# Attention by clusters and two feed-forward layers: a new order of units around the change of layers, and three roundings on another engine

## The chip, the cores and the metric

The program runs on one core of a Trainium2 chip. The metric is the device time of one execution in microseconds (us). The kernel before took 785.29, 785.1 and 782.73 us in three runs, median 785.1.

Engines are named as in the profile: PE is the matrix engine, DVE the vector engine, ACT the scalar engine, POOL is GpSimd, SP issues the DMAs.

## The reference

What is computed is an attention in which a query sees the keys of its own cluster alone, then two feed-forward layers on its 1536 rows of 512. Layer 2 normalizes its input and gates it.

```python
mask = q_assign[:, :, :, None] == k_assign[:, :, None, :]
scores = np.where(mask, scale * np.matmul(q, k.transpose(0, 1, 3, 2)), -1e9)
x = softmax(scores) @ v                      # 1536 rows of 512
h = x @ w_in                                 # layer 1: 512 to 2048
g = where(h >= 1, h, where(h <= -1, 0, (h + 1) ** 2 / 4))
x = g @ w_out                                # 2048 to 512
xn = x / sqrt(mean(x * x) + 1e-6) * rms_g    # layer 2
g = xn @ w_gate                              # 512 to 1536
out = (g / (1 + exp(-g)) * (xn @ w_val)) @ w_out
```

## The kernel before, in words

Every float32 product is made of three passes in a faster format. Each operand is split into a high part, rounded, and a low part, the remainder (`hi` and `low` in `rounded`, for a gated tile of 128 x 512). A product is high by high, high by low and low by high. Weights arrive in full and are split by DVE and ACT in six steps each (`conv_ops`), one step at a time between other work.

Tokens stand in three blocks b of 512, or twelve tiles t of 128. Hidden columns stand in slices m of 128, 16 in layer 1 and 12 in layer 2. Units of work on PE:

- `h_unit` (h): 12 matmuls of 512 columns, one slice m for one block b. ACT and DVE apply the gate, and `rounded` splits the result: high on ACT, low on DVE.
- `y_unit` (y): the second product of a group of slices for one tile of tokens, 9 matmuls for a group of three. DVE adds it to Y. The last group of layer 1 (n = 4, slices 13 to 15) also has ACT sum its squares.
- `norm_r` and `norm_y` (`norm` and `scale` in `units`): eleven small DVE instructions for a block's 1/rms, and one for each tile that scales Y.
- `turn_pair(t)` (pair): eight transposes, of tiles t and t + 4. ACT and DVE then make XH and XL, the high and low parts of layer 2's input, and three sums of the two blocks; the lows of these and of one quarter of the input are four instructions on POOL (L763).
- `turn_unit(t)` (turn): four transposes for a tile of block 2, with its high part on ACT and its low part on DVE (L865).

In layer 2, blocks 0 and 1 are multiplied by a scheme with seven products in place of eight. `term_unit(k, m)` is one of them, 6 matmuls, k from 1 to 7. Terms 1, 6, 7 and 4 add up in one accumulator B; ACT copies it away (u, v, w) between two of them, and the next may start only when the copy is done. Terms 5 and 3 share E, term 2 fills A. Terms 5 and 6 use the first of two sums of weights, 3 and 7 the second. These are made on POOL and split in two steps each. Block 2 takes the plain way (`one_unit`): `one(0, m)` is the gate product, `one(1, m)` the value product, 12 matmuls each. `slice_of(m)` lists, with the places freed left out: 1, 5, one(0), 2, 6, one(1), 3, 7. Term 4 of a slice (`last_of`) follows inside the next slice.

The order of units is written out by hand in `units`. Each engine executes its instructions in the order of the program. At the start of a unit `drain` issues the work behind the units before it, by stages, and `fill` adds steps of weight splitting as the planned times of PE and DVE allow (second and third entry of a unit). So a unit that is moved also moves its ACT, DVE and POOL work, and can move weight splitting and its loads. Weights pass through two load buffers: a load on SP waits until the splitting of the slice two before it is through.

Products and transposes share six banks of the accumulator memory in rotation (`HB`); a unit waits until the bank of six tiles before is read.

The hand order at the change of layers, layer 1's last group and layer 2's first slices:

Of the kernel before, what the change touches and what calls it, by code (L numbers as in the profile page):

```python
# [9 lines left out]
F32 = mybir.dt.float32  # L10
# [3 lines left out]
ALU = mybir.AluOpType  # L14
# [9 lines left out]
M1, M2 = FF1 // 128, FF2 // 128  # L24
TOK = B * S
BLK = 512
NB = TOK // BLK
GROUPS1 = [3, 3, 4, 3, 3]
# [12 lines left out]
def clustered_attention_two_ffn(  # L41
# [14 lines left out]
    nc = tc.nc  # L56
# [414 lines left out]
    a, b, c = prep(0), prep(1), prep(2)  # L471
# [27 lines left out]
    fp = {"gp": []}  # L499
# [127 lines left out]
    def h_unit(layer, m, b):  # L627
        cs = slice(BLK * b, BLK * b + BLK)
        w = need((layer, 0, m))
        drain()  # L630
        h = fp["h"](f"h{layer}_{m}_{b}")
        proj(h, w, cs)
        a = fp["a"](f"a{layer}_{m}_{b}")

        fp["g", m, b] = a
        G[layer, m, b] = take()

        def gate():
            nc.scalar.activation(a, h, AF.Relu, bias=half_b, scale=0.5)  # L639
            nc.scalar.activation(a, a, AF.Square)  # L640
            nc.vector.scalar_tensor_tensor(a, h, 1.0, a, op0=ALU.max, op1=ALU.min)  # L641

        hi, low = rounded(layer, m, b)
        later.append((gate, lambda: (hi(), low())))
# [15 lines left out]
    def rounded(layer, m, b):  # L660
        g = G[layer, m, b]

        def low():
            nc.vector.tensor_tensor(g[:, 1], fp["g", m, b], g[:, 0].bitcast(F32), op=ALU.subtract)
            whole.add((layer, m, b))

        return lambda: nc.scalar.copy(g[:, 0], fp["g", m, b]), low
# [26 lines left out]
    def key_of(k, m):  # L694
        i = TERMS[k][1]
        return (2, i, m) if i >= 0 else (2, -1 - i, -m - 1)
# [72 lines left out]
    def y_unit(layer, n, t):  # L769
        groups = (GROUPS1, GROUPS2)[layer - 1]  # L770
        m0 = sum(groups[:n])
        ms = range(m0, m0 + groups[n])
        b, j = divmod(t, 4)
        fs = slice(128 * j, 128 * j + 128)
        ws = [need((layer, layer, m)) for m in ms]
        drain()

        n_cols = 2 if layer == 2 and n + 1 == len(groups) and t == 3 else 1
        cols = [slice(DM // n_cols * c, DM // n_cols * (c + 1)) for c in range(n_cols)]
        ys = [fp["y"](f"y{layer}_{n}_{t}_{c}") for c in range(n_cols)]  # L780
        for c, y in zip(cols, ys):
            for m, w in zip(ms, ws):
                assert (layer, m, b) in whole
                g = G[layer, m, b]
                nc.tensor.matmul(y[:, c], g[:, 0, fs], w[:, 0, c], start=(m == m0), stop=False)  # L785
                nc.tensor.matmul(y[:, c], g[:, 0, fs], w[:, 1, c], start=False, stop=False)  # L786
                nc.tensor.matmul(y[:, c], g[:, 1, fs], w[:, 0, c], start=False, stop=(m == ms[-1]))  # L787
        if j == 3:
            for m in ms:
                give(G.pop((layer, m, b)))  # L790
        if t == (4 * NB - 1, 3)[layer - 1]:
            for m in ms:
                give(W.pop((layer, layer, m)))
        Y = fp["Y"][:, t]

        def add():
            for c, y in zip(cols, ys):
                if n == 0:
                    nc.scalar.copy(Y[:, c], y[:, c])
                else:  # L800
                    nc.vector.tensor_tensor(Y[:, c], y[:, c], Y[:, c], op=ALU.add)  # L801
                    tick()
                if n + 1 == len(groups):
                    if layer == 1:
                        norm_sq(t)
                    else:
                        nc.sync.dma_start(out[128 * t:128 * t + 128, c], Y[:, c])

        later.append((add,))
# [59 lines left out]
    def release(layer, m):  # L869
        for i in range(layer):  # L870
            give(W.pop((layer, i, m)))
# [4 lines left out]
    def units():  # L876

        def h(layer, m, b):
            return (lambda: h_unit(layer, m, b), 2.77, 1.36, [(1, 0, m)], -1)

        def y(layer, n, t):
            groups = (GROUPS1, GROUPS2)[layer - 1]
            m0 = sum(groups[:n])
            return (lambda: y_unit(layer, n, t), 0.693 * groups[n], 0.68 if n else 0.0,
                    [(layer, layer, m) for m in range(m0, m0 + groups[n])],
                    groups[n] * ((t % 4 == 3) + (t == (4 * NB - 1, 3)[layer - 1])))

        def done(layer, m):
            return (lambda: release(layer, m), 0.0, 0.0, [], layer)

        def turn(t):
            return (lambda: turn_unit(t), 0.6, 0.68, [], 0)

        def norm(b):
            return (lambda: norm_r(b), 0.0, 1.0, [], 0)

        def scale(t):
            return (lambda: norm_y(t), 0.0, 0.68, [], 0)

        def term(k, m):  # L900
            return (lambda: term_unit(k, m), 1.36, {2: 0.6, 3: 0.6, 7: 1.2, 4: 1.2}.get(k, 0.0), [key_of(k, m)], -(k in (7, 4)))

        def one(i, m):
            return (lambda: one_unit(i, m), 2.72, 1.2 * i, [(2, i, m)], -i)

        def end(*keys):
            return (lambda: free_unit(keys), 0.0, 0.0, [], len(keys))

        def slice_of(m):
            g, v, s, r = (2, 0, m), (2, 1, m), (2, 0, -m - 1), (2, 1, -m - 1)  # L910
            return [term(1, m), term(5, m), one(0, m), term(2, m), end(g), term(6, m), end(s), one(1, m), term(3, m), term(7, m), end(r)]

        def last_of(m):
            return [term(4, m), end((2, 1, m))]

        def ys(layer, n, b=None):
            return [y(layer, n, 4 * k + j) for k in ((2, 1, 0) if layer == 2 else range(NB)) for j in range(4) if b in (None, k)]

        def hs(layer, ms, b):
            return [h(layer, m, b) for m in ms]  # L920

        def scales(b):
            return [scale(t) for t in range(4 * b, 4 * b + 4)]

        def pair(t):
            return (lambda: turn_pair(t), 0.9, 2.2, [], -6 * (t == 0))

        def mix(xs, zs):
            r = []
            for i, x in enumerate(xs):  # L930
                r += [x] + zs[len(zs) * i // len(xs):len(zs) * (i + 1) // len(xs)]
            return r

        yield from [h(1, m, b) for b in range(NB) for m in range(GROUPS1[0])]
        for m in range(GROUPS1[0]):
            yield done(1, m)
        for n in range(1, len(GROUPS1) - 1):
            m0, g = sum(GROUPS1[:n]), GROUPS1[n]
            ks = []
            for m in range(m0, m0 + g):  # L940
                ks += [[h(1, m, b)] for b in range(NB)]
                ks[-1].append(done(1, m))
            for b in range(NB):
                yield from ys(1, n - 1, b)
                if n == 2 and b == 0:
                    yield (tables, 0.0, 0.0, [], 0)
                for k in ks[g * b:g * b + g]:
                    yield from k
        n = len(GROUPS1) - 1
        new = range(sum(GROUPS1[:n]), M1)  # L950
        yield from (*ys(1, n - 1, 0), *hs(1, new, 0), *ys(1, n - 1, 1), *hs(1, new, 1), *ys(1, n, 0))
        yield from mix(ys(1, n, 1), [norm(0), *scales(0)])
        ws = ys(1, n - 1, 2)
        yield from (ws[0], norm(1), ws[1], scale(4), ws[2], scale(5), ws[3], scale(6), scale(7))
        hz, yz = hs(1, new, 2), ys(1, n, 2)
        yield from (pair(0), *hz, *(done(1, m) for m in new), pair(1), pair(2), yz[0], yz[1], pair(3), yz[2], yz[3])
        zs = scales(2)
        f, e = slice_of(0), slice_of(1)
        yield from (f[0], f[3], norm(2), f[1], f[5], zs[0], f[6], zs[1], f[8], zs[2], e[0], f[9], zs[3], f[10], turn(8), e[1], turn(9),
                    *last_of(0)[:1], turn(10), e[3], turn(11), e[5], e[6], f[2], f[4], e[8], f[7], *last_of(0)[1:], e[2], e[4], e[9], e[10], e[7])  # L960
        for n, size in enumerate(GROUPS2):
            m0 = sum(GROUPS2[:n])
            for m in range(max(m0, 2), m0 + size):
                x = slice_of(m)
                yield from (*x[:2], *(last_of(m - 1) if m > m0 else ()), *x[2:])
            zs = ys(2, n)
            yield from (zs[0], *last_of(m0 + size - 1), *zs[1:])

# [105 lines left out]
    done = {"values": 4, "rows": []}  # L1074
# [259 lines left out]
```

## Time and profile before

| | before |
|---|---|
| median of three runs | 785.1 us |
| profiled execution, its own time | 783.73 us |
| its span, first to last instruction | 781.9 us |
| DVE busy over the span | 603.4 us (77%) |
| ACT busy | 391.8 us (50%) |
| POOL busy | 284.2 us (36%) |
| granted PE clock in the 40 slices | 0.9 or more of full speed in all |

The profiled execution has 1.8 us around its span, and lies 1.4 us below the median. Of a group or row of the trace the numbers are: start and duration in us from the first instruction, the engine, the line of the kernel, the operation, what it writes and reads, and in square brackets how long the engine stood idle before it and what ended that.

### The profile page before, as it was taken

How to read it: one execution, taken by the hardware profiler on the slowest of the kernel's cores; microseconds unless marked ns; L12 is line 12 of the kernel's file. 1: busy time of each engine (PE TensorE's matmuls, PEld its weight loads, DVE VectorE, ACT ScalarE, POOL GpSimd, SP SyncE). 2: the span in 40 equal slices, each digit the busy share in tenths (PEclk: the TensorE clock that was granted, in tenths of full speed). 3: DMA queues.
4: the chain of work that ended last, by engine and by line, in shares of the span. 5: the costliest groups of instructions: out<-in, count | busy, mean ns of one | idle time of the engine just before them, and what ended most of it. 6: DMA issues, size and time to landing. Idle time of an engine off the chain costs nothing.

```text
span 781.9 us, 10858 instructions
## 1 busy us (share of the span) xinstructions
PE 769.5 (98%) x3714; PEld 592.5 (76%) x3714; DVE 603.4 (77%) x1109; ACT 391.8 (50%) x758; POOL 284.2 (36%) x310
## 2 busy tenths in 40 slices
PE   8999999999999999999999998889999999999998
PEld 4666676666568888888888887678888888888887
DVE  6777787776678998877668779888999778988643
ACT  6676667665657555443334435554444314423420
POOL 5878999998000000000003214423455133432300
PEclk9999999999999999999999999999999999999999
DMA  7657665582153776444333300135463234343003
GB/s 199 173 138 182 153 165 125 137 203 80 62 160 132 231 253 199 162 135 140 116 120 137 108 28 27 55 102 167 165 213 135 81 128 141 137 134 108 1 37 125
DMA packets 32679, 103.41 MB, mean 132 GB/s; under 512 B 5016, under 2 KB 5356, under 8 KB 32624
## 3 DMA queue, kind: packets, MB, share of 16 engines
q1 hardware_dynamic: 32612, 102.72, 43.2%
q8 instruction: 29, 0.48, 0.2%
q14 instruction: 26, 0.21, 0.1%
q10 hardware_dynamic: 12, 0.00, 0.0%
HBM read 81.02 MB, written 3.15 MB: 108 GB/s over the span
## 4 chain that ended last, share of the span: by engine, by line
PE 93%; DVE 3%; ACT 2%; DMA 0%; issue 0%; POOL 0%; ACTq 0%; DVEq 0%
PE h L624 25%; PE y L785 9%; PE y L786 9%; PE y L787 9%; PE pv L406 8%; PE B L651 7%; PE mp L336 5%; PE sc L385 4%; PE sc L386 4%; PE E L651 4%; PE A L651 2%; PE sum L425 1%; PE simt L171 1%; PE sum L414 1%; PE warm L78 1%; DMA bb<-oht 0%
## 5 line engine op out<-in xcount | busy, mean ns | idle before, releaser
L338 DVE TENSOR_REDUCE M<-mp 128x1 f32<-128x384 f32 x186 | 94.6, 552 | 44.6 <-PE mp L336 44.4
L398 POOL TENSOR_TENSOR acc<-acc,P 128x384 f32<-128x384 f32 x112 | 109.3, 1010 | 4.1 <-ACT P L388 3.5
L388 ACT ACTIVATE P<-sc 128x384 f32<-128x384 f32 x192 | 82.3, 490 | 42.0 <-PE sc L386 36.1
L534 POOL TENSOR_TENSOR bits<-place 128x256 f32<-128x256 f32 x10 | 9.1, 934 | 256.0 <-DVE place L580 256.0
L624 PE MATMUL h<-xh,aa 128*128 128x512 f32 x312 | 99.9, 390 | 0.1
L801 DVE TENSOR_TENSOR Y<-y,Y 128x512 f32<-128x512 f32 (+1 forms) x85 | 57.7, 681 | 41.2 <-PE y L787 40.7
L639 ACT ACTIVATE a<-h,half_b 128x512 f32<-128x512 f32 x48 | 33.0, 688 | 81.9 <-PE h L624 80.8
L406 PE MATMUL pv<-P,v 128*64 128x384 f32 x384 | 70.6, 492 | 0.0
L624 PEld LDWEIGHTS h<-xh,aa 128*128 128x128 f32 x312 | 58.6, 188 | 14.2 <-DVE a L641 0.8
L385 PE MATMUL sc<-aa,bb 112*128 112x384 f32 x192 | 66.0, 344 | 0.0
L386 PE MATMUL sc<-aa,bb 97*128 97x384 f32 x192 | 65.0, 339 | 0.0
L624 PE MATMUL h<-xh,bb 128*128 128x512 f32 x200 | 64.4, 389 | 0.0
L565 ACT ACTIVATE raw<-raw 128x512 f32<-128x512 f32 x62 | 41.9, 677 | 40.1 <-DMA raw<-w_gate 23.3
L624 PE MATMUL h<-xl,aa 128*128 128x512 f32 x156 | 60.7, 389 | 0.0
L641 DVE SCALAR_TENSOR_TENSOR a<-h,a 128x512 f32<-128x512 f32 x48 | 33.1, 690 | 30.4 <-ACT a L640 30.4
L336 PE MATMUL mp<-bb,aa 112*128 112x384 f32 x186 | 52.4, 359 | 0.5 <-DMA bb<-oht 0.2
L568 DVE SCALAR_TENSOR_TENSOR bits<-raw,bits 128x512 uint32<-128x512 uint32 x68 | 50.0, 735 | 1.2
L406 PEld LDWEIGHTS pv<-P,v 128*64 128x64 f32 x384 | 25.4, 136 | 31.4 <-issue 30.5
L336 PEld LDWEIGHTS mp<-bb,aa 112*128 112x128 f32 x186 | 32.3, 189 | 15.9 <-issue 5.5
L624 PEld LDWEIGHTS h<-xh,bb 128*128 128x128 f32 x200 | 37.6, 188 | 7.8
L534 POOL TENSOR_TENSOR bits<-aa 128x256 f32<-128x256 f32 x18 | 17.6, 998 | 62.3 <-DVE aa L580 59.0
L624 PE MATMUL h<-xl,bb 128*128 128x512 f32 x100 | 38.9, 389 | 0.0
(306 smaller groups left out, 1944.5 us busy)
## 6 DMA issues: line engine op xcount, KB each, us to landing
raw<-w_out SPq DMA_DIRECT2D x28, 512.0 KB
mid<-w_out SPq DMA_DIRECT2D x28, 511.8 KB
raw<-w_in SPq DMA_DIRECT2D x16, 512.0 KB
mid<-w_in SPq DMA_DIRECT2D x16, 511.8 KB
raw<-w_gate SPq DMA_DIRECT2D x12, 512.0 KB
raw<-w_val SPq DMA_DIRECT2D x12, 512.0 KB
mid<-w_gate SPq DMA_DIRECT2D x12, 511.8 KB
mid<-w_val SPq DMA_DIRECT2D x12, 511.8 KB
```

The lines of the kernel that those rows point to most:

```text
L336: nc.tensor.matmul(mp, A[0:112, h, 0, 128 * qt:128 * qt + 128], Bk[0:112, h, 0, HALF * n:HALF * n + HALF], start=True, stop=True)
L338: nc.vector.tensor_reduce(st["M2", p][:, j, n:n + 1], mp, axis=AX.X, op=ALU.max)
L385: nc.tensor.matmul(sc, Bk[0:112, h, 0, ks], A[0:112, h, 0, qs], start=True, stop=False)
L386: nc.tensor.matmul(sc, Bk[0:97, h, 1, ks], A[0:97, h, 1, qs], start=False, stop=True)
L388: nc.scalar.activation(P, sc, AF.Exp, scale=0.125)
L398: nc.gpsimd.tensor_tensor(acc, acc, P, op=ALU.add)
L406: nc.tensor.matmul(pv[64 * h:64 * h + 64, 0:HALF], st["v", p][:, h, kt], st["P", p, i, h], start=(kt == 0), stop=(kt == NT - 1))
L624: nc.tensor.matmul(h, w[:, wi, fs], x[:, kc, cs], start=(n == 0), stop=(n == 11))
L651: nc.tensor.matmul(h, w[:, wi, fs], x[xi][:, kc], start=start and n == 0, stop=(n == 5), skip_group_check=not start)
L785: nc.tensor.matmul(y[:, c], g[:, 0, fs], w[:, 0, c], start=(m == m0), stop=False)
L786: nc.tensor.matmul(y[:, c], g[:, 0, fs], w[:, 1, c], start=False, stop=False)
L787: nc.tensor.matmul(y[:, c], g[:, 1, fs], w[:, 0, c], start=False, stop=(m == ms[-1]))
```

## The change

Three things. Layer 1's last three low parts of block 2 (slices 13 to 15) are subtracted on POOL in place of DVE. The units between the last products of layer 1 and the first slices of layer 2 stand in another order: h of block 2 comes first, and the pairs stand between the y units. In every slice of layer 2 from the third on, term 5 moves from second place to behind one(0) and term 2.

```diff
         def low():
-            nc.vector.tensor_tensor(g[:, 1], fp["g", m, b], g[:, 0].bitcast(F32), op=ALU.subtract)
+            e = nc.gpsimd if layer == 1 and b == NB - 1 and m >= M1 - GROUPS1[-1] else nc.vector
+            e.tensor_tensor(g[:, 1], fp["g", m, b], g[:, 0].bitcast(F32), op=ALU.subtract)
...
-        ws = ys(1, n - 1, 2)
-        yield from (ws[0], norm(1), ws[1], scale(4), ws[2], scale(5), ws[3], scale(6), scale(7))
-        hz, yz = hs(1, new, 2), ys(1, n, 2)
-        yield from (pair(0), *hz, *(done(1, m) for m in new), pair(1), pair(2), yz[0], yz[1], pair(3), yz[2], yz[3])
+        hz, ws, yz = hs(1, new, 2), ys(1, n - 1, 2), ys(1, n, 2)
+        yield from (hz[0], norm(1), scale(4), scale(5), hz[1], scale(6), scale(7), hz[2], *(done(1, m) for m in new), pair(0), ws[0], pair(1), ws[1], ws[2],
+                    pair(2), ws[3], yz[0], pair(3), yz[1], yz[2], yz[3])
...
-        yield from (f[0], f[3], norm(2), f[1], f[5], zs[0], f[6], zs[1], f[8], zs[2], e[0], f[9], zs[3], f[10], turn(8), e[1], turn(9),
-                    *last_of(0)[:1], turn(10), e[3], turn(11), e[5], e[6], f[2], f[4], e[8], f[7], *last_of(0)[1:], e[2], e[4], e[9], e[10], e[7])
+        yield from (f[0], f[3], f[1], norm(2), f[5], zs[0], f[6], zs[1], f[8], zs[2], e[0], f[9], zs[3], f[10], turn(8), e[3], turn(9),
+                    turn(10), e[1], turn(11), e[5], e[6], *last_of(0)[:1], e[8], f[2], f[4], e[9], e[10], f[7], *last_of(0)[1:], e[2], e[4], e[7])
...
-                yield from (*x[:2], *(last_of(m - 1) if m > m0 else ()), *x[2:])
+                yield from (*x[:1], *(last_of(m - 1) if m > m0 else ()), *x[2:5], x[1], *x[5:])
```

In the names below, `a1_15_2` is layer 1's gated tile of slice 15, block 2; `h1_13_2` its product, `y1_4_8` the y unit of layer 1, group 4, tile 8; `h0_0_2` is one(0) of slice 0; `xt`, `t` and `v` belong to the turns; `B4` is the accumulator B of slice 4. The last number is a running one.

DVE in the kernel before, between the last two gates of layer 1 and slice 15's low part:

```order
L641 SCALAR_TENSOR_TENSOR a1_15_2_5044<-h1_15_2_5031,a1_15_2_5044 128x512
L664 TENSOR_TENSOR place4_3132<-a1_14_2_5025,place4_3132 128x512
L755 TENSOR_TENSOR t1_0_5060<-v1_5062,xt1_5050 128x256
L755 TENSOR_TENSOR t1_0_5060<-xt5_5055,t1_0_5060 128x256
L755 TENSOR_TENSOR t1_1_5061<-xt5_5055,v1_5062 128x256
L755 TENSOR_TENSOR t1_1_5061<-xt1_5050,t1_0_5060 128x256
L756 TENSOR_TENSOR xl_104<-xt1_5050,xh_103 128x4x128
L757 TENSOR_TENSOR xl_104<-xt5_5055,xh_103 128x2x128
L664 TENSOR_TENSOR aa1_107<-a1_15_2_5044,aa1_107 128x512
```

The three low parts now, on POOL (L665), ahead of the lows of the first pair:

```order
L534 TENSOR_TENSOR bits37_4573<-bb1_108 128x256
L665 TENSOR_TENSOR aa1_107<-a1_13_2_4896,aa1_107 128x512
L665 TENSOR_TENSOR bb1_108<-a1_14_2_4926,bb1_108 128x512
L665 TENSOR_TENSOR bb0_106<-a1_15_2_4947,bb0_106 128x512
L764 TENSOR_TENSOR xl_104<-t0_0_4963,xh_103 128x2x128
L764 TENSOR_TENSOR aa2_109<-t0_0_4963,bb1_108 128x2x128
```

The low part of slice 15 stood behind a turn's six instructions on DVE, and stands behind its own two fellows on POOL now.

PE before, from the last turn of block 2 to the first unit that reads it, one(0) of slice 0:

```order
L858 MATMUL xt11_5349<-ident_f_68,Y_3125 128x128 x4
L651 MATMUL B1_5274<-bb0_106,bb1_108 128x512
L651 MATMUL B1_5274<-bb1_108 128x512
L651 MATMUL B1_5274<-bb0_106,bb1_108 128x512 x2
L651 MATMUL B1_5274<-bb1_108 128x512
L651 MATMUL B1_5274<-bb0_106,bb1_108 128x512
L624 MATMUL h0_0_2_5372<-xh_103,place3_3131 128x512
L624 MATMUL h0_0_2_5372<-xl_104,place3_3131 128x512
```

The same stretch of PE now, with the later rows of each unit left out:

```order
L859 MATMUL xt11_5315<-ident_f_68,Y_3125 128x128 x4
L651 MATMUL B1_5244<-bb1_108,place5_3133 128x512
...
L651 MATMUL B0_5183<-aa1_107,bb0_106 128x512
...
L651 MATMUL E1_5304<-xh_103,bb2_110 128x512
...
L624 MATMUL h0_0_2_5360<-xh_103,place3_3131 128x512
L624 MATMUL h0_0_2_5360<-xl_104,place3_3131 128x512
```

One term stood between the last turn and its reader; three stand there now.

PE before in layer 2, from the end of term 7 of slice 3 over terms 1 and 5 of slice 4 to term 4 of slice 3:

```order
L651 MATMUL B3_5834<-aa2_109,bb2_110 128x512
L651 MATMUL B4_5958<-xh_103,place4_3132 128x512
L651 MATMUL B4_5958<-xl_104,place4_3132 128x512
L651 MATMUL B4_5958<-xh_103,place4_3132 128x512 x2
L651 MATMUL B4_5958<-xl_104,place4_3132 128x512
L651 MATMUL B4_5958<-xh_103,place4_3132 128x512
L651 MATMUL E4_5971<-xh_103,place1_3129 128x512
L651 MATMUL E4_5971<-xl_104,place1_3129 128x512
L651 MATMUL E4_5971<-xh_103,place1_3129 128x512 x2
L651 MATMUL E4_5971<-xl_104,place1_3129 128x512
L651 MATMUL E4_5971<-xh_103,place1_3129 128x512
L651 MATMUL B3_5834<-place0_3128,bb0_106 128x512
```

The same place on PE now:

```order
L651 MATMUL B3_5813<-aa0_105,place4_3132 128x512
L651 MATMUL B4_5933<-xh_103,aa2_109 128x512
L651 MATMUL B4_5933<-xl_104,aa2_109 128x512
L651 MATMUL B4_5933<-xh_103,aa2_109 128x512 x2
L651 MATMUL B4_5933<-xl_104,aa2_109 128x512
L651 MATMUL B4_5933<-xh_103,aa2_109 128x512
L651 MATMUL B3_5813<-aa1_107,bb1_108 128x512
```

Two terms stood between terms 7 and 4 of a slice, and one stands there now; the copy w of the accumulator falls into this stretch.

## Rows read from the trace of the kernel before

**Rows 1.** Waits of PE from 440 us on: us in total, times, longest.

```profile
PE h L624 <- DVE xl L865: 2.0, 1, 2.0
PE y L787 <- DVE aa L664: 2.0, 1, 2.0
PE B L651 <- DVE xl L756: 1.0, 1, 1.0
PE xt L858 <- DVE Y L851: 0.6, 1, 0.6
PE B L651 <- ACT w L712: 0.5, 1, 0.5
PE B L651 <- ACT u L712: 0.3, 1, 0.3
PE y L785 <- ACT aa L667: 0.2, 1, 0.2
```

**Rows 2.** PE in order of time, at the change of layers.

```profile
462.21 0.39 PE L785 MATMUL y<-bb,place 128*128 128x512 f32 x1
464.25 0.39 PE L785 MATMUL y<-bb,place 128*128 128x512 f32 x1
...
483.42 0.40 PE L786 MATMUL y<-aa,aa 128*128 128x512 f32 x1
485.77 0.50 PE L787 MATMUL y<-aa,aa 128*128 128x512 f32 x1 [1.96 <-DVE aa L664]
486.11 0.40 PE L785 MATMUL y<-aa,place 128*128 128x512 f32 x1
...
488.17 1.03 PE L741 MATMUL xt<-ident_f,Y 128*128 128x128 f32 x8
488.96 0.48 PE L785 MATMUL y<-aa,place 128*128 128x512 f32 x1
...
520.14 0.39 PE L624 MATMUL h<-xh,bb 128*128 128x512 f32 x1
```

**Rows 3.** DVE in order of time, same stretch.

```profile
465.85 0.17 DVE L835 TENSOR_SCALAR ssq<-ssq 128x4 f32<-128x4 f32 x1 [0.25 <-ACT sq L829]
...
468.03 0.75 DVE L851 SCALAR_TENSOR_TENSOR Y<-Y,rr,gain 128x512 f32<-128x512 f32 x1
...
479.22 0.68 DVE L664 TENSOR_TENSOR place<-a,place 128x512 fp32r<-128x512 f32 x1
...
482.27 0.42 DVE L755 TENSOR_TENSOR t<-v,xt 128x256 f32<-128x256 f32 x1
...
484.76 0.96 DVE L664 TENSOR_TENSOR aa<-a,aa 128x512 fp32r<-128x512 f32 x1
...
492.22 0.42 DVE L755 TENSOR_TENSOR t<-v,xt 128x256 f32<-128x256 f32 x1 [2.83 <-ACT xh L751]
```

**Rows 4.** POOL in order of time, same stretch.

```profile
485.13 1.18 POOL L763 TENSOR_TENSOR bb<-t,bb 128x256 fp32r<-128x256 f32 x1
...
508.48 1.30 POOL L718 TENSOR_TENSOR w<-w,e 128x512 f32<-128x512 f32 x1 [5.12 <-ACT w L712]
```

**Rows 5.** ACT in order of time: a last gate, and a copy w in layer 2.

```profile
479.62 0.69 ACT L639 ACTIVATE a<-h,half_b 128x512 f32<-128x512 f32 x1 [0.53 <-PE h L624]
480.34 0.63 ACT L640 ACTIVATE a<-a 128x512 f32<-128x512 f32 x1
...
584.68 0.58 ACT L712 COPY w<-B 128x512 f32<-128x512 f32 x1
```

**Rows 6.** PE in order of time: the term 1 in whose time that copy falls.

```profile
584.06 0.39 PE L651 MATMUL B<-xh,place 128*128 128x512 f32 x1
```

**Rows 7.** Busy time by engine in one stretch of layer 2, with clock.

```profile
590.00:600.00 10.00, 10.00 (x46) 8.29 (x45) 9.90 (x18) 4.16 (x9) 4.88 (x6) 1.00 0.51 172
```

## The prediction

> **What bounds the kernel now.** I read the waits of PE from 440 us on first, then PE, DVE, POOL and ACT in order of time around each of them, then busy time by stretch. The waits say nearly all of it: in the last 342 us PE stands still seven times, 2.0 + 2.0 + 1.0 + 0.6 + 0.5 + 0.3 + 0.2 = 6.6 us, and all seven belong to the change of layers [rows 1]. In every other part of the feed-forward stage the end is set by the sheer number of matmuls, which the change leaves alone. So the change can win here and nowhere else, and it can lose wherever a unit comes closer to what it reads.
>
> Idle time is a little less than what a wait costs, since the matmuls beside it start slower too. Nine matmuls take 464.25 - 462.21 = 2.04 us, 0.227 each [rows 2]. Around the wait for slice 15's low part, three starts stand at 483.42, 485.77 and 486.11: 2.69 us in place of 0.45, which is 2.23 lost for an idle time of 1.96, 0.27 more [rows 2]. Seven waits at 0.27 more each make 6.6 + 1.9 = 8.5 us. A bound from above: from 462.21 to 520.14 PE does 192 matmuls (43.5 us) and 48 transposes (eight in 488.96 - 488.17 = 0.79, so 4.7 us) in 57.9 us, which leaves 9.7 us, part of it changeovers that stay [rows 2]. I take 8.5, with 6.6 and 9.7 as ends.
>
> **The change, wait by wait.** Up to the last y unit of block 1 the order of PE is the same, so both kernels reach 462.21 together. From there I count: 12 matmuls 2.72 us, 9 matmuls 2.04, 6 matmuls 1.36, a pair 0.79, a turn 0.40.
>
> 1. The low part of slice 15 (2.0 us, and the 0.2 for its high part). Before, only two pairs, 1.6 us, stand between h of slice 15 and the y unit that reads it, and on DVE a turn's six instructions (482.27 to 484.76, 2.49 us) stand ahead of the subtraction [rows 3]. Now h of slice 15 ends at 462.21 + 3 x 2.72 = 470.4, and its reader starts after three pairs and four y units, at 470.4 + 2.4 + 8.2 = 480.9. Gate and rounding on ACT and DVE are four instructions of 0.6 to 0.7 us [rows 3, 5]: 473.0. On POOL, the nearest row is an addition of the same size, 1.30 us [rows 4]; even three in a row end at 476.9. Four us of cover; the wait goes. The three subtractions that leave DVE, 0.68 us each [rows 3], are off the path in either place and count as nothing.
>
> 2. The low part of the last pair (1.0 us). Before, two y units stand between it and term 1 of slice 0; now three. Transposes end at 483.7; the copy to v on ACT first lets through the squares of tile 8, whose sum comes at about 484; a turn's ACT part (about 1.3 us) and its 2.49 us on DVE then end near 488 [rows 3]. Term 1 starts at 489.9. The wait goes with 2 us of cover.
>
> 3. Scaled Y for the first turn (0.6 us). The distance on PE is the same seven terms, 9.5 us. But DVE is no longer behind with pairs: the last sum of Y comes at about 490.5 in place of 496, the eleven small instructions take 468.03 - 465.85 = 2.18 us [rows 3], and even behind the sum for term 2 at 493.4 they end before 497, against 499.4 on PE. It goes.
>
> 4. The low part of the last turn (2.0 us). Before, one term of 1.36 us stands between the last turn and one(0), now three, 4.08 us. The 2.72 us more exceed what the wait cost, 2.2; it goes, with half a us over, and more because DVE comes to it earlier.
>
> 5. Copies u and w of slice 0 (0.3 and 0.5 us). w now has two terms more before term 4 and goes. u keeps its two terms, and its delay came from squares that ran late; I leave 0.3 in as the dear end.
>
> What is added: in seven places of layer 2 (slices 1, 3, 4, 6, 7, 9, 10) term 4 now comes one term, 1.36 us, behind term 7 in place of two. The copy w must fit in. The row of slice 3 ends 584.68 + 0.58 = 585.26, where the next term had begun at 584.06 [rows 5, 6]: 1.20 of the 1.36 us. Its own length, 0.58, leaves 0.78. So between -0.2 (a little later than that row) and 0.8 us of slack each: 0 to 1.4 us in all. I take 0.2, since the nearest row fits.
>
> Term 5 behind one(0) and term 2 gives its sum of weights 2.7 us more time; PE does not wait for it before, so it saves nothing by itself. The splitting of weights moves: the order puts 777 DVE instructions ahead of one(0) of slice 0 where 786 stood, 816 ahead of layer 2's first y unit where 830 stood, and 913 for 925 at the second group. Three of these are the moved ones; the rest, 6 to 11 steps of some 0.6 us, come later. So SP also issues the loads behind them later in the order, two buffers deep; PE needs these slices for the y units of layer 2 only, over 20 us on. I cost this at nothing; if that cover went, DVE would stand on a load and PE with it.
>
> Sum: 8.5 out, 0.3 + 0.2 left or new: 8.0 us. On the profiled execution's own time that is 783.73 - 8.0 = 775.7. That execution lay 1.4 below the median of the three runs, 785.1; the mean of the four is 784.2, and 784.2 - 8.0 = 776.2 is what I predict.
>
> **A rule against it.** DVE's subtraction of two operands in memory took 0.96 us at 484.76 while POOL worked, and 0.68 at 479.22; POOL's own 256 columns took 1.18 us beside it [rows 3, 4]. So the two slow each other by some 0.3 us, not by a whole instruction. The Trainium skill, SBUF — State Buffer, section "Who interferes with whom", says that a DVE instruction with two SBUF inputs contends with a GpSimd instruction that reads SBUF, and that the loser "**fully blocks** (not throttle)". By that rule three instructions of 1.30 us could hold DVE for 3.9 us. What hangs on it is the first rival; by the row it is 3 x 0.3 = 0.9 us, which the cover below hides.
>
> **Rivals.**
>
> A. The pairs become the bound. Six banks rotate, so the fourth tile after the first pair (the third y unit, at 476.0) needs the first pair read by DVE, which I place at 475.1: 0.9 us of cover, the least of all. If POOL's three subtractions hold DVE there for their whole length, 3 x 1.30 = 3.9 us [rows 4], 3.0 us come on PE; a DVE that waits for a copy of ACT as it did at 492.22, 2.83 us [rows 3], costs 1.9. For it: in the trace the pairs are where DVE and ACT wait for each other. Against: DVE has less ahead of it there now. Then 8.0 - 3.0 = 5.0 us are won: 779.2.
>
> B. It is handed back in layer 2. DVE is busy 9.90 of 10 us from 590 [rows 7]; if it works at its limit there, PE arrives 8 us early and waits for it. For it: that row. Against: the order puts 7 to 8 us less DVE work ahead of the same PE units, and PE's waits show none there [rows 1]. Then nothing is won: 784.2.
>
> C. The copy w decides, and it is slower. It stands on ACT behind the rounding of one(1)'s product, which waits for DVE. If DVE with its later splitting brings that 1.4 us later than in the row of slice 3, each of the seven places costs 1.4 - 0.16 = 1.24 us, 8.7 in all, over the 8.3 won before them: 784.2 + 0.4, and more for each tenth later; 2.0 us later make 4.6 us slower, 788.8. It decides from 1.35 us of lateness on. For it: it happens seven times. Against: at slice 3, in the densest stretch of DVE, the row still fits.
>
> D. The waits move to the first product terms instead of going (u, and POOL's lows of the last pair, which stand behind squares): some 2 us back, 778.2.
>
> **Numbers.** Forecast 0.68, with its own range 774 to 778; A 0.10, D 0.10, B 0.08, C 0.04. A run can lie 1.4 us to either side of the mean, so the low end is 776.2 - 2.0 = 774.2; the high end takes in A and a part of B, 781.2. Outside lie most of B and C and a little below, 2 in 10 at most. A difference under 0.3% (2.4 us) can't be told from none. Forecast, A and D are faster: 0.88. B is mostly within: 0.07. C and the rest slower: 0.05.
>
> **What would show it.** Right: the five waits for L664, L865, L756, L851 and w gone from PE's list, under 1 us of idle PE between the last y units of layer 1 and layer 2's first group; the three POOL subtractions done before 478; PE's one(0) of slice 0 starting without a wait. Wrong: a y unit that waits for DVE's read of a pair (A), PE waits on w behind term 1 from slice 2 on (C), or on a split of weights or a low part beyond 540 us (B).

## The result, and the profile after

The changed kernel takes 777.08 us (median of 6 runs, 775.71 to 778.5) against 785.05 us for the kernel before on the same chip (6 runs, 782.73 to 785.29): a ratio of 0.9903, 95% interval [0.9888, 0.9919]. Forecast were 776.2 us and a range of 774.2 to 781.2.

| | before | after |
|---|---|---|
| profiled execution, its own time | 783.73 us | 777.16 us |
| its span | 781.9 us | 775.3 us |
| DVE busy | 603.4 us (77%) | 609.2 us (79%) |
| ACT busy | 391.8 us (50%) | 392.0 us (51%) |
| POOL busy | 284.2 us (36%) | 289.3 us (37%) |

Waits of PE from 440 us on, after (total, times, longest, as in [rows 1]): of seven, one is left, and it is a new one.

```profile
PE E L651 <- DVE bb L559: 0.2, 1, 0.2
```

PE in order of time, before and then after (answering to [rows 2, 6]). The first row is the first matmul of layer 1, the last row the last matmul of all.

```profile
217.74 0.50 PE L624 MATMUL h<-xh,aa 128*128 128x512 f32 x1
...
778.53 0.28 PE L787 MATMUL y<-bb,aa 128*128 128x256 f32 x1
```

```profile
218.15 0.50 PE L624 MATMUL h<-xh,aa 128*128 128x512 f32 x1
...
490.65 0.39 PE L651 MATMUL B<-xh,place 128*128 128x512 f32 x1
...
500.17 0.60 PE L859 MATMUL xt<-ident_f,Y 128*128 128x128 f32 x4
...
502.00 1.03 PE L859 MATMUL xt<-ident_f,Y 128*128 128x128 f32 x8
503.04 0.50 PE L651 MATMUL E<-xh,place 128*128 128x512 f32 x1
...
505.02 0.66 PE L859 MATMUL xt<-ident_f,Y 128*128 128x128 f32 x4
...
508.03 0.39 PE L651 MATMUL B<-aa,bb 128*128 128x512 f32 x1
...
509.47 0.74 PE L651 MATMUL E<-xh,bb 128*128 128x512 f32 x2 [0.22 <-DVE bb L559]
...
510.51 0.40 PE L624 MATMUL h<-xh,place 128*128 128x512 f32 x1
...
577.19 0.39 PE L651 MATMUL B<-xh,aa 128*128 128x512 f32 x1
...
578.32 0.39 PE L651 MATMUL B<-xh,aa 128*128 128x512 f32 x1
...
579.26 0.62 PE L651 MATMUL B<-aa,bb 128*128 128x512 f32 x2
...
771.94 0.28 PE L788 MATMUL y<-aa,bb 128*128 128x256 f32 x1
```

From the first matmul of layer 1 to the last of all, PE took 560.79 us before and 553.79 after: 7.00 us less. The attention ahead of it took 0.41 us more, and the change does not touch it; so the two profiled executions differ by 6.57.

Two things are new. In slice 1 PE starts late without standing still for long. From 502.00 to 505.02 lie eight transposes and six matmuls, 3.02 us, where 0.79 + 1.36 would do: 0.87 lost. From 508.03 to 510.51 lie seven starts, 2.48 us in place of 1.59: 0.89 lost. And term 4 of slice 3, behind the matmul at 578.32, waits a little for the copy w: three starts to 579.26 take 0.94 in place of 0.68. On ACT the copy ends at 578.64, 1.45 us behind the start of the term at 577.19, where it had been 1.20 [rows 5, 6] and 1.36 are to be had:

```profile
578.06 0.58 ACT L713 COPY w<-B 128x512 f32<-128x512 f32 x1
```

POOL and DVE after, in order of time. First the first and the last of POOL's three low parts, then the last of its sums of weights of slice 1; then DVE (answering to [rows 3, 4]).

```profile
470.18 1.34 POOL L665 TENSOR_TENSOR aa<-a,aa 128x512 fp32r<-128x512 f32 x1 [22.25 <-ACT aa L668]
...
474.44 1.29 POOL L665 TENSOR_TENSOR bb<-a,bb 128x512 fp32r<-128x512 f32 x1 [0.26 <-ACT bb L668]
...
496.50 0.73 POOL L534 TENSOR_TENSOR s<-bits,bits 128x256 f32<-128x256 f32 x1
497.19 0.73 POOL L534 TENSOR_TENSOR s<-bits,s 128x256 f32<-128x256 f32 x1
```

```profile
475.17 0.68 DVE L757 TENSOR_TENSOR xl<-xt,xh 128x512 fp32r<-128x512 f32 x1
...
488.49 0.68 DVE L757 TENSOR_TENSOR xl<-xt,xh 128x512 fp32r<-128x512 f32 x1
...
495.04 0.70 DVE L836 TENSOR_SCALAR ssq<-ssq 128x4 f32<-128x4 f32 x1
...
496.59 0.66 DVE L840 TENSOR_TENSOR rt<-rt,ssq 128x4 f32<-128x4 f32 x1
...
497.98 0.16 DVE L839 SCALAR_TENSOR_TENSOR rt<-rr 128x4 f32<-128x4 f32 x1
...
499.16 2.08 DVE L852 SCALAR_TENSOR_TENSOR Y<-Y,rr,gain 128x512 f32<-128x512 f32 x3
...
503.02 0.79 DVE L559 TENSOR_TENSOR place<-s,place 128x512 fp32r<-128x512 f32 x1 [0.58 <-ACT place L557]
...
509.66 0.68 DVE L866 TENSOR_TENSOR xl<-xt,xh 128x512 fp32r<-128x512 f32 x1
```

The eleven small instructions of block 2's norm run from 495.04 to 499.16: 4.12 us, where 2.18 had been read [rows 3]. The slow ones (0.58 to 0.70, four of them) lie beside POOL's sums, and each ends within 0.04 us of the end of a POOL instruction: the one at 496.59 ends at 497.25, POOL's of 496.50 at 497.23. From 497.98 on, where POOL is done, each takes 0.16 again. Behind them stand the scaling of tiles and the split of slice 1's sum of weights (503.02), for which term 5 (503.04) waits; that split itself waits 0.58 us for ACT's cast. The last row is the last turn's low part.

### The profile page after: what moved, and what is told of

It is laid out like the page before. It is cut to its first block, busy times and chain, and to the rows that moved or that the text cites. A ratio compares the mean times of both kernels' runs of the same rounds, so it can differ in the third digit from the quotient of the medians.

```text
span 775.3 us, 10868 instructions
## 1 busy us (share of the span) xinstructions
PE 768.0 (99%) x3714; PEld 592.2 (76%) x3714; DVE 609.2 (79%) x1106; ACT 392.0 (51%) x758; POOL 289.3 (37%) x313
## 4 chain that ended last, share of the span: by engine, by line
PE 92%; DVE 3%; ACT 2%; POOL 1%; DMA 1%; issue 1%; SPq 0%; ACTq 0%; DVEq 0%; POOLq 0%
PE h L624 25%; PE y L787 9%; PE y L788 9%; PE y L786 9%; PE pv L406 8%; PE B L651 7%; PE mp L336 5%; PE sc L385 4%; PE sc L386 4%; PE E L651 4%; PE A L651 2%; PE sum L425 1%; PE simt L171 1%; PE sum L414 1%; DMA bb<-oht 1%
## 5 line engine op out<-in xcount | busy, mean ns | idle before, releaser
L534 POOL TENSOR_TENSOR bits<-place 128x256 f32<-128x256 f32 x18 | 17.6, 998 | 265.6 <-DVE place L580 265.6
L624 PE MATMUL h<-xh,aa 128*128 128x512 f32 x280 | 89.2, 390 | 0.1
L624 PEld LDWEIGHTS h<-xh,aa 128*128 128x128 f32 x280 | 52.6, 188 | 12.8 <-DVE a L641 0.8
L624 PE MATMUL h<-xl,aa 128*128 128x512 f32 x140 | 54.5, 389 | 0.0
L568 DVE SCALAR_TENSOR_TENSOR bits<-raw,bits 128x512 uint32<-128x512 uint32 x68 | 51.7, 760 | 1.6
L719 POOL TENSOR_TENSOR w<-w,e 128x512 f32<-128x512 f32 x12 | 17.1, 1423 | 61.3 <-ACT w L713 61.3
```

The lines of the kernel that those rows point to most:

```text
L624: nc.tensor.matmul(h, w[:, wi, fs], x[:, kc, cs], start=(n == 0), stop=(n == 11))
```

## The experiments

Theory at the start: the gain is the waits at the change of layers that went, and the two new orders are the parts that took them away. Rivals: the low parts on POOL or the later term 5 carry it, or part of it is clock.

**The four parts alone.** The order around layer 1's last group:

```diff
+        yield from (hz[0], norm(1), scale(4), scale(5), hz[1], ..., pair(2), ws[3], yz[0], pair(3), yz[1], yz[2], yz[3])
```

> Only the order at the end of layer 1 is new (h of block 2 first, the pairs between the y units). Low parts stay on DVE, slices 0 and 1 and term 5 stay as before. My theory (order alone gives the distance): the waits for the low part of slice 15 (2.0 us), its high part (0.2), the last pair's low part (1.0) and scaled Y (0.6) go, 3.8 us idle and 0.27 more for each, so 4.9 us faster, 780.2 of 785.1; the wait for the last turn's low part (2.0) stays. Rival (the move to POOL is what removes the first wait): it stays at about 2 us and the gain is 2.5 us, 782.6.

Measured 780.09 us, ratio 0.9949 [0.9931, 0.9966] to the kernel before at 784.23: 4.1 us faster where 4.9 were expected, which the interval takes in. The wait for L664 is gone; the wait for xl L865 (1.9 us) stays, and the one for Y L851 grew from 0.6 to 1.4, and term 5 of slice 1 waits 1.3 for its split sum of weights.

The order of slices 0 and 1:

```diff
+        yield from (f[0], f[3], f[1], norm(2), ..., turn(8), e[3], turn(9),
+                    turn(10), e[1], turn(11), e[5], e[6], *last_of(0)[:1], ...)
```

> Only the order of slices 0 and 1 is new (three terms between the last turn and one(0), w with two terms more). My theory: the waits for the last turn's low part (2.0 us) and w (0.5) go, 2.5 us idle and 0.27 more for each, so 3.0 us faster, 782.1 of 785.1; the three waits before it stay (low of slice 15 2.0, last pair 1.0, scaled Y 0.6). Rival (DVE is still behind with the pairs, so the wait moves to the first sum of weights of slice 1): 1 us faster at most, 784.

Measured 780.32 us, 0.9949 [0.9931, 0.9967]: 3.9 us faster where 3.0 were expected; the 782.1 was reckoned from 785.1. Of PE's long waits only the 2.0 us for L664 stays.

Term 5 behind one(0) and term 2, in the later slices alone:

```diff
+                yield from (*x[:1], *(last_of(m - 1) if m > m0 else ()), *x[2:5], x[1], *x[5:])
```

> Only term 5 moves behind one(0) and term 2, in the slices of layer 2 from the third on. My theory: no gain, since PE waited for no sum of weights there, and at most a wait of 0.2 us on the copy w at a place or two: within 0.3 us of 785.1. Rival (w decides at all seven places): 1.2 us at each, 8 us slower.

Measured 784.4 us, 1.0006 [0.9991, 1.002]: nothing, and PE's seven waits are those of before.

The three low parts on POOL alone:

```diff
+            e = nc.gpsimd if layer == 1 and b == NB - 1 and m >= M1 - GROUPS1[-1] else nc.vector
```

> Only the three low parts move to POOL, the order is that of before. My theory: slice 15's low part no longer stands behind a turn on DVE, but its y unit still follows two pairs behind: it starts at the rounding (483.1) and takes 1.3 us, 484.4 for 485.7, so the wait of 2.0 us falls to 0.7 and the gain is 1.3 to 2 us, 783.4. Rival (the new order makes the distance and the engine is indifferent): under 0.5 us.

Measured 783.38 us, 0.9985 [0.9974, 0.9997]: 0.85 us, where 1.3 to 2 were expected. The 2.0 us for L664 became waits of 0.6 and 0.4 us for POOL's low parts, and the wait for the last pair grew from 1.0 to 1.4. The single gains, 4.1 + 3.9 - 0.2 + 0.9, add up to 8.7, a little over the whole. By that the later term 5 does nothing and the other parts simply add. The next run shows that they do not.

**Both orders, without POOL and term 5.**

```diff
+        hz, ws, yz = hs(1, new, 2), ys(1, n - 1, 2), ys(1, n, 2)
...
+        yield from (f[0], f[3], f[1], norm(2), ...)
```

> The kernel before with both new orders of units together (around layer 1's last group, and in layer 2's first two slices), the three low parts left on DVE and term 5 of the later slices left in second place. Theory: the two orders are the whole change, since low parts on POOL alone and term 5 alone won 0.9 us and nothing. Then the time is that of the changed kernel within 0.5 us, about 7.5 to 8 us under the kernel before (776.3 to 777.3), PE shows no wait over 0.5 us at the change of layers, and its granted clock is 1.000. Rival: the low parts on POOL are needed with the orders, since DVE then takes the pairs 0.68 us per subtraction later and the pairs stand close to what reads them; then PE waits for a pair or for slice 15's low part, and it is 1 us or more slower than the changed kernel.

Measured 779.73 us, 0.9947 [0.9934, 0.9961] to 784.59 before. The theory is wrong: together the orders win 4.9 us, hardly more than one of them alone. The waits at the change of layers are gone; from slice 2 of layer 2 on, four waits for split sums of weights stand, 1.1, 1.0, 0.3 and 0.2 us. Two parts were left out of this kernel, and the next pair tells which one matters.

**The change without one of the two.** First term 5 back in second place:

```diff
-                yield from (*x[:1], *(last_of(m - 1) if m > m0 else ()), *x[2:5], x[1], *x[5:])
+                yield from (*x[:2], *(last_of(m - 1) if m > m0 else ()), *x[2:])
```

> The changed kernel with term 5 of the later slices back in second place; both new orders and the three low parts on POOL stay. Theory (once the stalls at the change of layers are gone, PE comes to layer 2 so early that term 5 in second place stands before its sum of weights is split; the 1.10 us wait in slice 4 of the run with the two orders alone is this): 2 to 2.7 us slower than the changed kernel, 779.1 to 779.8, with PE waits of about 1 us for splits of the first sum of weights beyond 580 us. Rival (the low parts on POOL are what that run lacked): within 0.5 us of the changed kernel, no such wait.

Then the low parts back on DVE:

```diff
-            e = nc.gpsimd if layer == 1 and b == NB - 1 and m >= M1 - GROUPS1[-1] else nc.vector
+            e = nc.vector
```

> The changed kernel with the three low parts of layer 1 back on DVE; both new orders and the later term 5 stay. Theory (term 5 is what the run with the two orders alone lacked, and the low parts are off the path in either place, as I costed them): within 0.5 us of the changed kernel. Rival (the low parts on POOL give DVE the 2 us by which it keeps ahead in layer 2): 2 to 2.7 us slower than the changed kernel.

And the change as it is, beside them:

> The changed kernel as it is, to have it beside the others on one chip: 776.5 to 777.7, granted clock 1.000 in all runs, 7 to 8 us under the kernel before.

The change takes 776.18 us here, 0.9902 [0.9887, 0.9917] to 783.85 before. Without the low parts on POOL it takes 776.25, 0.9908 [0.9893, 0.9923]: no difference. With term 5 in second place it takes 780.74, 0.9961 [0.9947, 0.9974]: 4.6 us come back, more than the theory's 2 to 2.7. Waits of PE in that kernel, but for the 0.2 us for bb in slice 1 that the changed kernel has too:

```profile
PE E L651 <- ACT aa L557: 1.1, 1, 1.1
PE E L651 <- DVE place L559: 1.0, 1, 1.0
PE E L651 <- ACT place L557: 0.3, 1, 0.3
PE E L651 <- DVE aa L559: 0.2, 1, 0.2
```

DVE, ACT and PE of that kernel in order of time, around term 5 of slice 5, which waits longest (the expectation took it for slice 4):

```profile
590.68 0.42 DVE L578 TENSOR_SCALAR bits<-bb 128x512 uint32<-128x512 uint32 x1
...
593.14 0.69 DVE L576 SCALAR_TENSOR_TENSOR place<-raw,bits 128x512 fp32r<-128x512 f32 x1
593.74 0.69 DVE L676 TENSOR_TENSOR a<-h,a 128x512 f32<-128x512 f32 x1
594.46 0.62 ACT L668 CAST aa<-a 128x512 fp32r<-128x512 f32 x1 [3.10 <-DVE a L676]
594.99 0.58 ACT L713 COPY w<-B 128x512 f32<-128x512 f32 x1
595.47 0.60 ACT L672 ACTIVATE a<-E 128x512 f32<-128x512 f32 x1
595.96 0.62 ACT L557 CAST aa<-s 128x512 fp32r<-128x512 f32 x1
...
596.63 0.50 PE L651 MATMUL E<-xh,aa 128*128 128x512 f32 x1 [1.15 <-ACT aa L557]
```

On POOL the last addition to that sum ends at 587.82 + 1.19 = 589.01:

```profile
587.82 1.19 POOL L534 TENSOR_TENSOR s<-bits,s 128x256 f32<-128x256 f32 x1
```

The sum is ready 7 us before its cast. The cast stands on ACT behind the rounding of one(1)'s product, the copy w and a gate. The rounding waits 3.10 us for DVE's multiplication of that product with its gate (593.74), and ahead of this DVE goes through six steps of weight splitting, from 590.68 on. The busy share of DVE does not tell the kernels apart: from 560 to 580 us it is 19.41 of 20 us here and 19.31 in the kernel before.

In the kernel before, cast and subtraction of the same sum stand far ahead of the copy w (599.50) in the order, and term 5 reads them 10 us later:

```profile
587.52 0.62 ACT L557 CAST aa<-s 128x512 fp32r<-128x512 f32 x1
...
589.54 0.69 DVE L559 TENSOR_TENSOR aa<-s,aa 128x512 fp32r<-128x512 f32 x1
...
599.50 0.58 ACT L712 COPY w<-B 128x512 f32<-128x512 f32 x1
...
600.38 0.39 PE L651 MATMUL E<-xh,aa 128*128 128x512 f32 x1
```

In the changed kernel the cast is as late as in the one without the move: it runs 376.4 us behind the first matmul of layer 1, there 376.6, and before 369.8. But term 5 now stands behind term 4, one(0) and term 2, 1.36 + 2.72 + 1.36 = 5.44 us later, and its split is through 1.4 us ahead of it:

```profile
594.52 0.63 ACT L557 CAST place<-s 128x512 fp32r<-128x512 f32 x1
...
596.63 1.23 DVE L559 TENSOR_TENSOR place<-s,place 128x512 fp32r<-128x512 f32 x1
...
599.23 0.39 PE L651 MATMUL E<-xh,place 128*128 128x512 f32 x1
```

So with the new orders the cast runs some 6.6 us later. PE, on the other hand, comes sooner: without the move it is ready for term 5 at 595.32, 375.9 us behind the first matmul of layer 1, where it had been 382.6 (600.38). The two together use up the 12.9 us that lay between cast and term in the kernel before, and the later term 5 makes room again. The other waits belong to term 5 as well, at 526.26 in slice 2, and at 666.88 and 668.62 in slice 8. Matmul starts lose 0.5 us at slice 2, 1.7 at slice 5 and 1.9 at slice 8, and the 0.26 for the copy w is saved: 3.8 us. From the first matmul of layer 1 to the last, 219.41 to 777.10, this kernel takes 557.69 us, 3.90 more than the changed one. What the other 0.7 of the 4.6 between the medians is stays open; the parts of a run ahead of layer 1 differ by more than that, 217.74 to 219.41.

The same stretch, from the first matmul of layer 1 to the last of all, in the profiled executions, one of each kernel and two of the change (that of the new slices alone holds the stretch at a lower clock that is shown further down):

| kernel | us | less than before |
|---|---|---|
| before | 560.79 | |
| order at the end of layer 1 alone | 557.95 | 2.84 |
| order of slices 0 and 1 alone | 557.69 | 3.10 |
| term 5 alone | 560.81 | -0.02 |
| low parts on POOL alone | 559.91 | 0.88 |
| both orders | 557.89 | 2.90 |
| both orders, low parts on POOL | 557.69 | 3.10 |
| both orders, term 5 | 554.03 | 6.76 |
| the change | 553.79, 553.79 | 7.00 |

With both orders in place, the move of term 5 is worth 3.86 us without the low parts on POOL and 3.90 with them; these are worth 0.2 us in either case.

**The clock.** Eight matmuls that add zeros in each of the two places where PE stood for 2 us:

```diff
+    def nothing(t, n):
+        for _ in range(n):
+            nc.tensor.matmul(t, zeros, zeros.unsqueeze(1).to_broadcast([128, 4, 128]), start=False, stop=False)
...
+                if filled and n == 1:
+                    nothing(h, 8)
```

> The kernel before with eight more matmuls that add zeros to the same accumulator (8 x 0.22 = 1.8 us) in each of the two places where PE stood still for 2 us: ahead of the third pass of layer 1's last group for tile 8, and ahead of the second pass of one(0) of slice 0. The two stalls are filled with work, the time that PE needs for what it waits for is unchanged. Theory (part of the gain is the clock, which is granted at its lower level for some 3 us after such a stall in some executions): the granted clock is 1.000 in all runs and the time is 782.5 to 783.3, 1 to 2 us under the kernel before with its runs at 0.995 to 1.000. Rival (the stalls cost only their idle time, and the clock varies for another reason): runs spread over the same 782.4 to 787 as before, median 784.2 to 785, granted clock as low as 0.995 in some.

All 12 runs have a mean granted clock of 0.999 or 1.000, as the theory said; of the 22 runs of before beside them 14 lie at 0.995 to 0.997. So the lower clock comes from the stalls, since it is gone where they are filled. The time is 783.93 us, 0.9991 [0.9982, 1.0001]: 0.66 us, less than the 1 to 2 expected, and the interval touches none. Over all 56 runs of before in the three sets of experiments, the 20 with 0.999 or more average 783.4 us, the other 36 784.9. That a part of the change's gain is clock, some 1 us of the average run (36 of 56 times 1.5), is argued from which runs go together; the filled kernel alone does not show it. What the clock does after a stall is seen in the profile of the kernel with the new slices alone, PE in order of time and the stretch with its clock:

```profile
483.40 0.40 PE L786 MATMUL y<-aa,aa 128*128 128x512 f32 x1
485.77 0.50 PE L787 MATMUL y<-aa,aa 128*128 128x512 f32 x1 [1.96 <-DVE aa L664]
...
487.40 0.63 PE L787 MATMUL y<-aa,place 128*128 128x512 f32 x1
...
489.11 1.71 PE L741 MATMUL xt<-ident_f,Y 128*128 128x128 f32 x8
490.58 0.48 PE L785 MATMUL y<-aa,place 128*128 128x512 f32 x1
```

```profile
480.00:500.00 20.00, 17.70 (x79) 13.81 (x77) 15.38 (x31) 13.00 (x36) 9.51 (x12) 0.91 0.02 3
```

Behind the 1.96 us of idle, from 487.40 on, matmuls start 0.43 us apart in place of 0.23 and eight transposes take 1.47 in place of 0.79: PE runs at 1.2 and not 2.4 GHz until about 490.5, which is what a mean of 0.91 over these 20 us says too (0.09 x 20 x 2 = 3.6 us at half the clock). Late as PE then is, its 1.0 us wait for the last pair does not show in that kernel.

**The small instructions of the norm.** In the changed kernel, POOL's sums of slice 1 issued ahead of the last pair's lows:

```diff
         def low():
+            while t == 3 and fp["gp"]:
+                fp["gp"].pop(0)()
```

> The changed kernel with one thing more: POOL's sums of weights of slice 1 are issued ahead of POOL's low parts of the last pair and not behind them, so that they do not run beside the norm of block 2 on DVE. Theory (the eleven small instructions of that norm take 4.12 us and not 2.18 because POOL adds tiles beside them, and that is what makes PE start 1.4 us late in slice 1): the eleven take about 2.2 us, the waits for the split sum of weights and for the last turn in slice 1 go, and it is 1.2 to 1.4 us faster than the changed kernel, 775.7. Rival (the starts in slice 1 are late because ACT's casts are late, or the low parts of the last pair now come later and B waits for them): within 0.5 us of the changed kernel, or slower.

Measured 779.04 us, 0.9928 [0.9914, 0.9942]: 2 us slower than the change, though the first half of the theory holds. The rows of the norm, and PE's waits:

```profile
500.50 0.16 DVE L838 TENSOR_SCALAR ssq<-ssq 128x4 f32<-128x4 f32 x1
...
502.48 0.16 DVE L843 SCALAR_TENSOR_TENSOR rr<-rt,rr 128x4 f32<-128x4 f32 x1
```

```profile
PE xt L861 <- DVE Y L854: 1.2, 2, 0.7
PE B L651 <- ACT u L713: 1.0, 1, 1.0
```

With POOL idle, each takes 0.16 us again, 2.14 together. But the earlier sums brought their splits ahead of the norm on DVE and ACT, so the norm begins at 500.50 in place of 495.04 (4.2 us later, counted from the first matmul of layer 1), and the turns wait for it.

The planned DVE time of that norm, as the trace had it:

```diff
-            return (lambda: norm_r(b), 0.0, 1.0, [], 0)
+            return (lambda: norm_r(b), 0.0, 4.0 if b == 2 else 1.0, [], 0)
```

> The changed kernel with the planned DVE time of the norm of block 2 at 4 us in place of 1, what it took in the trace, so that the planner puts two steps of weight splitting behind it and not beside it. Theory (DVE is late in slice 1 by the sum of the slow norm and the steps planned beside it): 0.7 to 1 us faster than the changed kernel, 776.2, and the sum of weights for term 5 split earlier. Rival (the steps must be done there anyway, and only move the lateness on): within 0.4 us of the changed kernel.

Measured 782.06 us, 0.9968 [0.9959, 0.9978]: 5 us slower than the change, worse than both expectations. Splitting did go behind the norm, and what went was wanted at once:

```profile
PE E L651 <- ACT place L557: 3.2, 1, 3.2
```

A second wait, 1.1 us for the copy w of slice 3, is new as well. The granted clock is 0.997 or 0.998 in all ten runs: here too a long stall, 3.2 us, goes with clock lost.

**The cast for term 5 of slice 1 earlier.**

```diff
-        yield from (..., zs[1], f[8], zs[2], e[0], f[9], zs[3], ...)
+        yield from (..., zs[1], f[8], e[0], zs[2], f[9], zs[3], ...)
```

> The changed kernel with the scaling of tile 10 one unit later, behind term 1 of slice 1 and not ahead of it. With it the high cast of slice 1's first sum of weights is issued on ACT ahead of the gate that waits for DVE's addition to E. Theory (the cast at 502.38 us stands behind that gate, which idles ACT for 2.23 us, and the split after it makes term 5 of slice 1 start late): the cast runs before 500 us, term 5 of slice 1 starts without a wait, 0.4 to 0.7 us faster than the changed kernel. Rival (DVE sets it, since the low half of the split keeps its place behind three other instructions on DVE, or the turn of tile 10 now waits): within 0.3 us of the changed kernel, or slower.

Measured 776.42 us, 0.9905 [0.9891, 0.992], against 776.18 for the change beside it: no difference. The cast ran at 495.51 as wanted and term 5's wait went, but term 3 of slice 1 now waits 0.7 us for ACT's copy e. No version beat the change.

## Why the prediction was right, and where it was not

**The five waits** all went, most of them with about the covers that were worked out. POOL's three low parts ended at 474.44 + 1.29 = 475.7 (bound 476.9); the last pair's low part came at 489.2 (near 488), 1.5 us ahead of term 1 at 490.65 (489.9); one(0) of slice 0 starts 0.23 us behind the matmul before it. Wait 3 went narrowly: the first scaling ends at 499.9 and the first turn starts at 500.17, 0.3 us of cover where the prediction had 2.4 (497 against 499.4), since the norm took longer. Wait 4 was near too: the last turn's low part ends at 510.34, the matmul that reads it starts at 510.75, and PE was 1.76 us late by then. Wait 1 owes this to the order alone: with the low parts on DVE the time is the same, as their cost of nothing in either place had it.

**The sum.** Predicted were 8.5 us out and 0.5 left, 8.0. The feed-forward part won 7.00. Late starts of 0.87 + 0.89 in slice 1 and 0.26 for w are new, so what went is 7.00 + 2.02 = 9.0 us: between the 8.5 and the upper end, 9.7. The price of a wait with its 0.27 held; the term that was mis-sized is what is left or new, 0.5 predicted and 2.0 measured. Of it the copy w took its part, 0.26 for 0.2, and at one place of the seven. The copy u cost nothing; the 1.76 of slice 1 was not in the sum. Ahead of it on DVE stands step 3's norm, whose eleven small instructions got 2.18 us from a row with POOL idle and took 4.12. That PE would start on time with a quicker norm was not shown: the run that made it quick also moved it.

**The rule that was set aside** (by the row: 0.3 us for each of POOL's instructions) is borne out in just that place. Small instructions of 0.16 us took 0.66 beside POOL instructions of 0.73 and ended with them, so they are held until the POOL instruction is through. The Trainium skill, SBUF — State Buffer, section "Who interferes with whom", calls the ports that the two engines share an exclusive lock, and says for DVE's modes with two ports that the loser is blocked, not throttled; for these instructions the trace agrees.

**The clock** was not in the prediction. It took the profiled execution, at a granted clock of 1.000, as one draw among four that lay 1.4 us under the median. The runs show what it goes with: executions of before at 0.999 or 1.000 average 783.4 us. Against them the ten runs of the change (six of 777.04 and four of 776.14 on average, 776.7) win 6.7 us, and the other 1.3 of the 7.97 between the medians goes with the clock. The filled stalls gave 0.66 of it, at the edge of the noise, so its size is argued and not shown. That the gain of 8.0 was met so closely is luck: two errors offset each other, some 1.3 us too much for what the new order wins at one clock, and about as much clock left out. The 0.9 us between forecast and result are the base: 784.2 was taken, 785.05 measured.

**The failed step** is term 5, "it saves nothing by itself", with the splitting of weights, "I cost this at nothing". Alone the move does save nothing (1.0006). Together with the new orders it holds 3.9 of the 7.0 us of the profiled stretch, 4.6 of the 7.7 between the medians. The splitting that the orders push back was costed for layer 2's y units, over 20 us on; among it are the cast and the subtraction of the sum of weights that term 5 reads, and term 5 is the nearest reader. So rival B, handed back in layer 2, is what happens without the move, and it argued from the right row, DVE at its limit before 600 us [rows 7]; after, the same stretch has 9.27 in place of 9.90. The argument against it, fewer DVE instructions ahead of the same PE units, counted work that had not gone but moved behind.

**The other rivals.** A did not occur: the first pair's low part on DVE ended at 475.85, 0.75 later than placed, without a wait on PE. C did not: w costs 0.26 us once. D did not: the first terms of slice 0 start on time.

## What to carry to other kernels

A part of a change that gains nothing alone can be what holds the gain of the rest: test each part by taking it out of the whole, too. Work that an order pushes back is free only if its first reader, through every sum and split between, is far enough off. Read the duration of small instructions at the place where they will run, beside the engine that runs there.

## What was not expected of the hardware

The same stall of PE, 1.96 us, was followed by a granted clock of 0.91 in the stretch from 480 to 500 us in one profile (the new slices alone), and by 1.00 in that of the kernel before. Over its runs the mean clock of before is 0.995 to 1.000, and 783.4 or 784.9 us go with it. Four DVE instructions of 4 columns took 0.58 to 0.70 us beside POOL's additions, each up to the end of one, and 0.16 without them.
